# Scores of the last half block: two pairs to a bank, two teams in place of four

## The chip, the cores and the metric

The kernel runs on one core of one Trainium2 chip. The metric is the device time of one execution in microseconds (us). Engines are named as the profile names them: PE (TensorE matmul), PEld (its weight loads), DVE (VectorE), ACT (ScalarE), POOL (GpSimd), SP (SyncE, which issues most DMAs). Times written without a unit are microseconds from the start of the span.

## The reference

An attention without softmax feeds a mixture of experts whose router takes the best expert and keeps the first 768 tokens of each.

```python
scores = scale * np.matmul(z, z.transpose(0, 2, 1))        # 8 batches x 3072 x 3072, d_qk = 64, scale = 1 / 3072
attn = np.maximum(scores, 0.0) ** 2
x = u * np.matmul(attn, v)                                 # 24576 tokens x 256
...
logits = x @ w_gate                                        # 8 experts
expert_idx = np.argmax(logits, axis=1)
...
# the first capacity = 768 tokens of an expert, in order of the tokens, are kept; all others give rows of zeros
h = np.maximum(np.einsum('ecd,edf->ecf', disp, w1), 0.0)   # 256 -> 1024
y = np.einsum('ecf,efd->ecd', h, w2)                       # 1024 -> 256
out[i] = gate_w[i] * y[expert_idx[i], pos[i]]
```

## The kernel before

Numbers are carried as pairs of f16 (a high part and the rest), so that a product is three matmuls: high x high, high x rest, rest x high.

**Attention.** Only as many tokens are computed as fill the experts: 13 blocks of 512 queries and a last half block of 256, numbered 0 to 13. A block's keys come in 12 pairs of 128-key tiles. For a pair that isn't kept from an earlier block (scores are symmetric), `team` makes the scores with matmuls of 64 rows (`zz` by `zz` into the PSUM tiles `sc`, three for each tile, the two tiles of a pair on the two halves of the PE array), and `follow` lays out what happens to them: ACT takes the relu out of PSUM (`r`), ACT squares it (`a`), DVE casts the square to f16 and subtracts to get the rest (`hl`). The sums (`acc`) then take 12 matmuls of 256 columns for a pair of a half block. The tag `sc` has six banks of PSUM. Scores are made ahead of the sums for a team of pairs at a time, at most `TEAM = 3`, one bank for each tile; the list `teams` holds them in order, and `scores_to` starts a team when the sums come within two or three pairs of it. In block 13 pairs 0 and 1 are turned scores of block 12 (`nx`) and pairs 2 to 11 are computed: ten pairs.

**Routing.** When a block's sums are done, `drain` multiplies them by `u` (`x`), and `route` splits x into f16 parts (`rm`, `rse` ... for the scale, then `xr`), turns them with DMA transposes (`xt`), takes the logits on PE (`lg`, which takes one of the six banks too), counts slots (`cum`) and scatters the rows (`disp`) from POOL. Block 12 is routed while block 13 is computed, block 13 under the first expert's work.

**Experts.** A slab of an expert's rows is loaded (`fxt`, `meta`). For each of 8 groups of hidden columns PE makes `hps` in the banks of tag `sc`, and ACT and then DVE write its two f16 parts (`hh`). Then PE makes `yps`, which ACT and DVE scale (`ys`) and POOL scatters to `out`. The first slab has 640 rows in two halves of 384 and 256, so its hidden work is 16 groups of 6 matmuls; a bank comes free when DVE has written the group's `hh`. Weights are loaded (`wraw`), their largest value found (`wm`, an all-reduce on POOL, then `w1e` to `winv`) and split (`wt`). Expert 1's weights are prepared during block 13 and the first slab. Zero rows of the output are written between (`zero`).

**Order.** Nothing is scheduled on the chip: each engine runs its list in order. The list is made by the program itself: the PE work is written out in sequence, and `weave` puts in the steps of all waiting chains by an estimate of the engines' clocks (`clk`, with the costs written beside each step), the chain's rank, and conditions such as "six `hl` buffers". A change of one step's place or cost can therefore move steps of other chains on DVE, ACT and SP.

```python
blocks = [(bats[n // BPB], n % BPB, 0, CC if n < NB0 - 1 else CC // 2) for n in range(NB0)]
```

Of the kernel before, what the change touches and what calls it, by code (L numbers as in the profile page):

```python
# [9 lines left out]
F32 = mybir.dt.float32  # L10
# [8 lines left out]
P = 128  # L19
BLK = 512  # L20
MROW = 8
NHL = 6
TEAM = 3
# [5 lines left out]
def attention_moe_kernel(ctx: ExitStack, tc: tile.TileContext, u, v, z, w_gate, w1, w2, out, cap):  # L29
    nc = tc.nc  # L30
    B, S, D = u.shape
    DQ = z.shape[2]
# [4 lines left out]
    NPAIR = JT // 2  # L37
    BPB = S // BLK
    NBLK = B * BPB
    CC = BLK // P  # L40
# [11 lines left out]
    ps = ctx.enter_context(tc.tile_pool(name="ps", bufs=2, space=PSUM))  # L52
# [142 lines left out]
    def op(eng, cost, dep=0.0):  # L195
        start = max(clk[eng], dep + HOP)
        if eng in ("SP", "XB"):
            start = max(clk["SP"], dep + HOP)
            clk["SP"] = start + (0.5 if eng == "SP" else max(1.2, 0.3 + cost))
            clk["DMA"] = max(clk["DMA"], start + 1.4) + cost  # L200
            return clk["DMA"] + 1.0
        clk[eng] = start + cost
        return clk[eng]
# [64 lines left out]
    def weave():  # L268
        more_ = True
        while more_:  # L270
            more_ = watch()
            for c in list(chains):
                while c.fits():
                    c.emit()
                    more_ = True
                if c.item() is None:
                    chains.remove(c)

    def need(*keys):

        for k in keys:
            n = 0
            while k not in done:
                weave()
                if k not in done:
                    clk["PE"] += 0.1
                    n += 1
                    assert n < 100000, k
        return max((done[k] for k in keys), default=0.0)
# [573 lines left out]
    def attention(blocks, hook):  # L863
# [19 lines left out]
        def at(p):  # L883
            n, i = divmod(p, NPAIR)
            return n, 2 * order[n][i // 2] + i % 2

        def is_kept(p):
            n, g = at(p)
            bt, ib, _, _ = blocks[n]
            return (g // 2, ib) in bt.kept  # L890

        def is_next(p):


            n, g = at(p)
            bt, ib, _, _ = blocks[n]
            return (g // 2, ib) in bt.follows
# [8 lines left out]
        def cornered(p):  # L906


            n, g = at(p)
            _, ib, _, cc = blocks[n]  # L910
            return n > 0 and cc == CC and g == 2 * ib + 1


        computed = [p for p in range(NP) if not is_kept(p) and not is_next(p)]
        place = {p: i for i, p in enumerate(computed)}
        opening = hasattr(blocks[0][0], "to_scores")
        k = 6 if opening else 0
        teams = deque(tuple(computed[i:i + 2]) for i in range(0, k, 2))
        teams.extend(tuple(computed[i:i + TEAM]) for i in range(k, len(computed), TEAM))
        loads = deque(p for p in range(NP) if is_kept(p))  # L920

        def load(p):
# [12 lines left out]
        def team(ps_):  # L935

            made = []
            while small[0]:  # L940
                weave()
                clk["PE"] += 0.1 if small[0] else 0.0
            latest[:] = [0, *((aid, "r", place[p]) for p in ps_)]
            op("PE", 0.205)
            for p in ps_:
                n, g = at(p)
                bt, ib, c0, cc = blocks[n]
                t = need(bt.key("z", 2 * g // 4), bt.key("z", ib))
                if place[p] >= TEAM:
                    t = max(t, need((aid, "r", place[p] - TEAM)))  # L950
                w, q0 = cc * P, ib * BLK + c0 * P
                if cornered(p):
                    w, q0 = HB, q0 + HB
                s = [ps.tile([P, BLK], F32, tag="sc", name="sc", bufs=6) for _ in range(2)]
                for i, (kl, ql) in enumerate(((0, 0), (0, 1), (1, 0))):
                    for jj in (0, 1):
                        rows, j = slice(DQ * jj, DQ * (jj + 1)), 2 * at(p)[1] + jj
                        nc.tensor.matmul(s[jj][:, 0:w], lhsT=bt.zz[rows, (kl + jj) % 2, j * P:(j + 1) * P],  # L958
                                         rhs=bt.zz[rows, (ql + jj) % 2, q0:q0 + w], start=(i == 0), stop=(i == 2))
                t = op("PE", 3 * w / 2400, t)  # L960
                made.append(follow(p, s, w, t))
            return made

        def follow(p, s, w, t):
# [73 lines left out]
        def scores_to(p):  # L1038
            while teams and due() <= p:
                team(teams.popleft())  # L1040
# [52 lines left out]
        bt = blocks[0][0]  # L1093
        if hasattr(bt, "to_scores"):
            bt.to_scores()
            del bt.to_scores
            ahead = deque(teams[1])
            bt.to_sums(team(teams.popleft()), lambda: team((ahead.popleft(),)))
            teams.popleft()
        else:  # L1100
            scores_to(0)
        clear[0] = open_bank
        operand = {}
        for p, c in steps():
            where[:] = p, c
            n, g = at(p)
            bt, ib, c0, cc = blocks[n]
            i = p % NPAIR
# [18 lines left out]
            if i == 0 and c % 2 == 0:  # L1127

                k = bank[0] - 2
# [6 lines left out]
            for jj in (0, 1):  # L1136
                j = 2 * g + jj


                for h, l in ((0, 0), (0, 1), (1, 0)):  # L1140
                    nc.tensor.matmul(o, lhsT=a(h, jj, c), rhs=bt.v2[:, j, l], start=(i + jj + h + l + c % 2 == 0),  # L1141
                                     stop=(i == NPAIR - 1 and jj + h == 2), skip_group_check=True)
# [233 lines left out]
    with tc.manual_schedule():  # L1376
# [5 lines left out]
        for b, bt in bats.items():  # L1382
            n = min(BPB, NB0 - b * BPB)
# [55 lines left out]

        blocks = [(bats[n // BPB], n % BPB, 0, CC if n < NB0 - 1 else CC // 2) for n in range(NB0)]  # L1440
        attention(blocks, hook)
        done["attended"] = clk["PE"]
        cn = last_route[0][1]
# [16 lines left out]
        with tc.If(flag > 0):  # L1460
            nb, ib0 = divmod(NB0, BPB)

            def tail(b, ibs, half=()):
                go_on = nc.values_load(more, min_val=0, max_val=1)
                with tc.If(go_on > 0):
                    bt = batch(b)
                    prepare(bt)
                    attention([(bt, ib, CC // 2, CC // 2) for ib in half] + [(bt, ib, 0, CC) for ib in ibs],
                              lambda p: None)
                    finish()  # L1470
                    check_full()
                    finish()

            if ib0:
                tail(nb, range(ib0, BPB), [ib0 - 1])
                nb += 1
            else:
                tail(nb - 1, [], [BPB - 1])
            if nb < B:
                with tc.For_i(nb, B, 1) as b:  # L1480
                    tail(b, range(BPB))
            with tc.For_i(0, E, 1) as e:
                experts([e])
                finish()
# [25 lines left out]
```

## Time and profile before

| What | Value |
|---|---|
| Median of three runs | 777.61 us (776.28 to 780.22) |
| The profiled execution | 778.41 us, of which its span is 776.5 us |
| PE busy | 766.8 us, 99% of the span |
| DVE, ACT, POOL busy | 514.4, 401.1, 116.6 us |
| Block 13, from its first scores to the first `hps` | 494.54 to 519.49 |
| Hidden work of the first slab | 519.49 to 532.65 |

The span runs from the first to the last instruction of the profiled execution; its time is 1.9 us longer. In a row of the timeline the columns are the start, the time taken, the engine, the line, the operation, out<-in, the shapes and the count, and in brackets the idle time before it with what ended it. Ends of matmuls are modelled, so the time of PE's work is best read from one row's start to the next row's.

### The profile page before, as it was taken

How to read it: one execution, taken by the hardware profiler on the slowest of the kernel's cores; microseconds unless marked ns; L12 is line 12 of the kernel's file. 1: busy time of each engine (PE TensorE's matmuls, PEld its weight loads, DVE VectorE, ACT ScalarE, POOL GpSimd, SP SyncE). 2: the span in 40 equal slices, each digit the busy share in tenths (PEclk: the TensorE clock that was granted, in tenths of full speed). 3: DMA queues.
4: the chain of work that ended last, by engine and by line, in shares of the span. 5: the costliest groups of instructions: out<-in, count | busy, mean ns of one | idle time of the engine just before them, and what ended most of it. 6: DMA issues, size and time to landing. Idle time of an engine off the chain costs nothing.

```text
span 776.5 us, 16291 instructions
## 1 busy us (share of the span) xinstructions
PE 766.8 (99%) x6474; PEld 572.3 (74%) x6474; DVE 514.4 (66%) x1134; ACT 401.1 (52%) x690; POOL 116.6 (15%) x122
## 2 busy tenths in 40 slices
PE   9999999999999999999999999999999999999996
PEld 3777878888887787878888877876666656666664
DVE  7998789754308799875554268889576575575741
ACT  6985558433016667573530057675455464463541
POOL 0000020210202020202022020203320321313302
PEclk9999999999999999999999999999999999999999
DMA  7699949999978979698789949882898955944001
GB/s 224 124 351 137 288 104 241 178 220 195 189 149 166 326 177 228 164 235 190 166 153 197 201 134 214 305 233 58 236 264 286 319 147 215 296 120 185 28 15 45
DMA packets 283831, 149.49 MB, mean 193 GB/s; under 512 B 229742, under 2 KB 255675, under 8 KB 283745
## 3 DMA queue, kind: packets, MB, share of 16 engines
q1 hardware_dynamic: 278848, 135.57, 71.8%
q0 software_dynamic: 4896, 12.79, 5.3%
q8 instruction: 52, 0.85, 0.4%
q14 instruction: 35, 0.28, 0.1%
HBM read 36.25 MB, written 59.92 MB: 124 GB/s over the span
## 4 chain that ended last, share of the span: by engine, by line
PE 88%; issue 3%; DMA 3%; DVE 2%; POOL 1%; SPq 1%; ACT 0%; POOLq 0%; ACTq 0%; DVEq 0%
PE acc L1141 51%; PE hps L1287 14%; PE yps L1311 14%; PE sc L958 8%; DMA ld<-kept 2%; DMA vraw<-in_v 1%; POOL out L86 1%; PE lg L722 1%; DVE hl L993 1%; SPq L375 0%; DVE hl L984 0%; DVE wm L75 0%; DVE xr L707 0%; DVE v L527 0%; SPq L369 0%
## 5 line engine op out<-in xcount | busy, mean ns | idle before, releaser
L1141 PE MATMUL acc<-v,hl 128*128 128x256 f16 x2280 | 260.7, 273 | 1.0 <-DVE v L527 0.6
L1141 PEld LDWEIGHTS <-hl 128*128 128x128 f16 x2280 | 219.5, 98 | 36.4 <-issue 9.2
L975 ACT ACTIVATE r<-sc 128x512 f32<-128x512 f32 (+1 forms) x212 | 105.5, 550 | 142.2 <-PE sc L958 140.0
L1311 PE MATMUL yps<-wt,hh 128*128 128x256 f16 (+1 forms) x776 | 126.8, 324 | 0.0
L1287 PE MATMUL hps<-fxt,wt 128*128 128x384 f16 (+2 forms) x816 | 126.7, 317 | 0.0
L993 DVE TENSOR_TENSOR hl<-a,hl 128x1024 f16<-128x1024 f32 (+1 forms) x106 | 118.1, 1114 | 3.5
L1287 PEld LDWEIGHTS <-wt 128*128 128x128 f16 x816 | 77.8, 98 | 47.1
L1311 PEld LDWEIGHTS <-hh 128*128 128x128 f16 x776 | 75.7, 98 | 48.4
L86 POOL DMA_INDIRECT disp<-xr,slot x54 | 56.8, 1051 | 359.7 <-issue 215.5
L1141 PE MATMUL acc<-v,ld 128*128 128x256 f16 x960 | 109.0, 273 | 0.6 <-DMA ld<-kept 0.6
L980 ACT ACTIVATE a<-r 128x1024 f32<-128x1024 f32 (+1 forms) x106 | 102.6, 968 | 5.0 <-DVE hl L993 2.6
L1141 PEld LDWEIGHTS <-ld 128*128 128x128 f16 x960 | 92.7, 98 | 13.9 <-issue 2.1
L984 DVE CAST hl<-a 128x1024 f16<-128x1024 f32 (+1 forms) x106 | 67.5, 637 | 45.8 <-ACT a L980 45.0
L1273 DVE SCALAR_TENSOR_TENSOR hh<-hps,hh 128x384 f16<-128x384 f32 (+2 forms) x136 | 70.6, 530 | 34.6 <-ACT hh L1272 33.1
L1272 ACT ACTIVATE hh<-hps 128x384 f16<-128x384 f32 (+2 forms) x136 | 63.4, 470 | 48.9 <-PE hps L1287 47.3
L86 POOL DMA_INDIRECT out<-ys,sid x48 | 53.3, 1111 | 129.9 <-DVE ys L1320 77.1
L958 PE MATMUL sc<-zz 64*128 64x512 f16 (+1 forms) x636 | 68.5, 355 | 0.0
L704 ACT ACTIVATE xr<-x,rsr 128x256 f16<-128x256 f32 x54 | 24.4, 500 | 82.9 <-DVE rsr L62 66.7
L1317 ACT ACTIVATE ys<-yps,sg 128x256 f32<-128x256 f32 x48 | 22.7, 474 | 76.9 <-PE yps L1311 70.4
L1320 DVE SCALAR_TENSOR_TENSOR ys<-yps,sg,ys 128x256 f32<-128x256 f32 x47 | 22.7, 483 | 53.0 <-ACT ys L1317 50.6
L1141 PE MATMUL acc<-v,nx 128*128 128x256 f16 x504 | 57.4, 273 | 0.0
L1141 PEld LDWEIGHTS <-nx 128*128 128x128 f16 x504 | 49.0, 98 | 6.5 <-issue 0.8
(135 smaller groups left out, 485.7 us busy)
## 6 DMA issues: line engine op xcount, KB each, us to landing
out<-zero SPq DMA_DIRECT2D x48, 512.0 KB
kept<-hl SPq DMA_DIRECT2D x40, 512.0 KB
wraw<-in_moe_w SPq DMA_DIRECT2D x32, 512.0 KB
vraw<-in_v SPq DMA_DIRECT2D x18, 512.0 KB
u<-in_u SPq DMA_DIRECT2D x13, 512.0 KB
zraw<-in_z SPq DMA_DIRECT2D x2, 768.0 KB
zz<-zz SPq DMA_DIRECT2D x4, 384.0 KB
xt<-xr SPq DMA_TRANSPOSE x54
```

Of the source, the lines that this page charges most:

```text
L86: r = nc.gpsimd.indirect_dma_start(out=dst, out_offset=bass.IndirectOffsetOnAxis(ap=idx, axis=0), in_=src, in_offset=None, bounds_check=bo ...
L704: return lambda: nc.scalar.activation(st.x16[:, c, 0:D], st.x[:, c, :], AF.Copy, scale=st.rs[:, c:c + 1])
L958: nc.tensor.matmul(s[jj][:, 0:w], lhsT=bt.zz[rows, (kl + jj) % 2, j * P:(j + 1) * P], rhs=bt.zz[rows, (ql + jj) % 2, q0:q0 + w], start=(i ...
L975: nc.scalar.activation(sct[p][:, jj, :], s[jj][:, 0:w], AF.Relu)
L980: nc.scalar.activation(sq[p], sct.pop(p), AF.Square)
L984: nc.vector.tensor_copy(hl[:, :, :, 0, :], sq[p].rearrange("p j (t k) -> p j t k", k=HB))
L993: nc.vector.tensor_sub(hl[:, :, :, 1, :], a.rearrange("p j (t k) -> p j t k", k=HB), hl[:, :, :, 0, :])
L1141: nc.tensor.matmul(o, lhsT=a(h, jj, c), rhs=bt.v2[:, j, l], start=(i + jj + h + l + c % 2 == 0), stop=(i == NPAIR - 1 and jj + h == 2), sk ...
L1272: Chain([[("ACT", 0.05 + w * 0.00083, lambda: nc.scalar.activation(th, src, AF.Relu), None)], [("DVE", 0.07 + w * 0.00104, lambda: nc.vect ...
L1273: [("DVE", 0.07 + w * 0.00104, lambda: nc.vector.scalar_tensor_tensor(out=tl, in0=src, scalar=0.0, in1=th, op0=ALU.max, op1=ALU.subtract), ...
L1287: nc.tensor.matmul(o, lhsT=wx.w1[:, d, wp, f * P:(f + 1) * P], rhs=sx.xt[:, xp * DC + d, a:a + w], start=(q == 0), stop=(q == len(seq) - 1))
L1311: nc.tensor.matmul(y[:, 0 if end else l], lhsT=hid(i, f)[:, sl], rhs=w[:, l], start=(f + i == 0 and l != 1), stop=(f == FC - 1 and i == 1) ...
```

## The change

In the half block two pairs share two banks: the first tiles of both lie side by side in one bank of 2 x 256 columns, the second tiles in another. The matmuls of the two pairs are interleaved (all three products of both), the first of a bank clears it. A team may then hold twice as many pairs as six banks allowed before, and the ten pairs are made in two teams of five. Full blocks keep their teams; their tiles are given the width that they use.

```diff
-        teams.extend(tuple(computed[i:i + TEAM]) for i in range(k, len(computed), TEAM))
+        full = sum(blocks[p // NPAIR][3] == CC for p in computed)
+        if full > k:
+            teams.extend(tuple(computed[i:min(i + TEAM, full)]) for i in range(k, full, TEAM))
+        k = -(-(len(computed) - full) // (2 * TEAM))
+        n = -(-(len(computed) - full) // max(k, 1))
+        teams.extend(tuple(computed[i:i + n]) for i in range(full, len(computed), max(n, 1)))
...
-                s = [ps.tile([P, BLK], F32, tag="sc", name="sc", bufs=6) for _ in range(2)]
+                if cc == CC:
+                    s = [ps.tile([P, 1, w], F32, tag="sc", name="sc", bufs=6) for _ in range(2)]
+                    two = [(p, 0)]
+                elif ps_.index(p) % 2 == 0:
+                    s = [ps.tile([P, 2, w], F32, tag="sc", name="sc", bufs=6) for _ in range(2)]
+                    two = [(x, y) for y, x in enumerate(ps_[ps_.index(p):ps_.index(p) + 2])]
+                else:
+                    two = []
                 for i, (kl, ql) in enumerate(((0, 0), (0, 1), (1, 0))):
-                    for jj in (0, 1):
-                        rows, j = slice(DQ * jj, DQ * (jj + 1)), 2 * at(p)[1] + jj
-                        nc.tensor.matmul(s[jj][:, 0:w], lhsT=bt.zz[rows, (kl + jj) % 2, j * P:(j + 1) * P],
-                                         rhs=bt.zz[rows, (ql + jj) % 2, q0:q0 + w], start=(i == 0), stop=(i == 2))
-                t = op("PE", 3 * w / 2400, t)
-                made.append(follow(p, s, w, t))
+                    for x, y in two:
+                        for jj in (0, 1):
+                            rows, j = slice(DQ * jj, DQ * (jj + 1)), 2 * at(x)[1] + jj
+                            nc.tensor.matmul(s[jj][:, y], lhsT=bt.zz[rows, (kl + jj) % 2, j * P:(j + 1) * P],
+                                             rhs=bt.zz[rows, (ql + jj) % 2, q0:q0 + w], start=i + y == 0, stop=i == 2,
+                                             skip_group_check=True)
+                for x, y in two:
+                    made.append(follow(x, [z[:, y] for z in s], w, op("PE", 3 * w / 2400, t)))
```

Up to the half block every engine's list is as it was. From there the planner places other chains differently. Two places matter for what follows.

On SP, while block 13 is computed, the list before has expert 1's weights (`wraw`) ahead of the first slab (`fxt`), and then the turning of block 12's rows (`xt`):

```order
L1071 DMA u<-in_u 128x4x256
L1399 DMA out<-zero 256x1x512 x3
L1172 DMA wraw<-in_moe_w 128x1024 x2
L1174 DMA wraw<-in_moe_w 128x4x256 x2
L1399 DMA out<-zero 256x1x512
L1241 DMA_TRANSPOSE fxt<-disp 128x4x640
L1242 DMA meta<-disp 128x5x8
L1399 DMA out<-zero 256x1x512 x3
L715 DMA_TRANSPOSE xt<-xr 128x4x128 x4
```

The same place of the list after the change:

```order
L1085 DMA u<-in_u 128x4x256
L1413 DMA out<-zero 256x1x512 x3
L1255 DMA_TRANSPOSE fxt<-disp 128x4x640
L1256 DMA meta<-disp 128x5x8
L1186 DMA wraw<-in_moe_w 128x1024 x2
L1188 DMA wraw<-in_moe_w 128x4x256 x2
L1413 DMA out<-zero 256x1x512 x2
L715 DMA_TRANSPOSE xt<-xr 128x4x128 x2
```

The slab, which waits for the scatters of block 11, now stands ahead of the four weight loads, and the loads stand ahead of the turning of block 12's rows.

On DVE, around the first hidden groups of the first slab, the list before goes from the end of block 13 (`x<-acc`) over the seven small steps for expert 1's scale to the first `hh`, and has the routing of block 13 between the groups:

```order
L1080 TENSOR_TENSOR x<-acc,u 128x512
L60 TENSOR_SCALAR w1e<-wma 128x1
L62 TENSOR_SCALAR w1i<-w1e 128x1
L62 TENSOR_SCALAR w1r<-w1i 128x1
L60 TENSOR_SCALAR w2e<-wma 128x1
L62 TENSOR_SCALAR w2i<-w2e 128x1
L62 TENSOR_SCALAR w2r<-w2i 128x1
L1198 TENSOR_TENSOR winv<-w1i,w2i 128x1
L1273 SCALAR_TENSOR_TENSOR hh<-hps,hh 128x384
L1273 SCALAR_TENSOR_TENSOR hh<-hps,hh 128x256
L692 TENSOR_REDUCE rm<-x 128x2
```

After the change the seven steps come first, then `x<-acc`, and then these rows; the first `hh` stands behind the routing steps of block 13 up to `xr` and two splits of expert 1's weights:

```order
L692 TENSOR_REDUCE rm<-x 128x2
L60 TENSOR_SCALAR rse<-rm 128x2
L62 TENSOR_SCALAR rsi<-rse 128x2
L62 TENSOR_SCALAR rsr<-rsi 128x2
L60 TENSOR_SCALAR rf<-rsi,cb 128x2
L60 TENSOR_SCALAR rfg<-rsi,cbg 128x2
L1228 SCALAR_TENSOR_TENSOR wt<-wraw,w1r,wt 128x512
L770 COPY xr<-tokid 128x2x4
L60 TENSOR_SCALAR tokid<-tokid 128x4
L1228 SCALAR_TENSOR_TENSOR wt<-wraw,w1r,wt 128x512
L707 SCALAR_TENSOR_TENSOR xr<-x,rsr,xr 128x256 x2
L1287 SCALAR_TENSOR_TENSOR hh<-hps,hh 128x384
```

Behind the first `hh` now come the six steps on block 12's logits (`lgs` to `oh`), which before stood ahead of `x<-acc`. On PE the logits of block 12 (`lg`, 16 matmuls) moved from the last sums of block 13 to behind the second hidden group, and those of block 13 (8 matmuls) from the `yps` work into the ninth group.

## Rows read from the trace of the kernel before

**Rows 1.** The page, parts 1 and 2: PE's busy time, granted clock.

```profile
PE 766.8 (99%) x6474; PEld 572.3 (74%) x6474; DVE 514.4 (66%) x1134; ACT 401.1 (52%) x690; POOL 116.6 (15%) x122
PEclk9999999999999999999999999999999999999999
```

**Rows 2.** The timeline of PE in block 13 and the first slab.

```profile
494.54 1.16 PE L958 MATMUL sc<-zz 64*128 64x256 f16 x18
495.63 4.10 PE L1141 MATMUL acc<-v,hl 128*128 128x256 f16 x36
499.57 2.78 PE L1141 MATMUL acc<-v,nx 128*128 128x256 f16 x24
...
512.69 0.50 PE L958 MATMUL sc<-zz 64*128 64x256 f16 x6
513.12 4.53 PE L1141 MATMUL acc<-v,hl 128*128 128x256 f16 x38
...
518.76 0.55 PE L722 MATMUL lg<-wg,xt 128*128 128x16 f16 x16
519.16 0.49 PE L1141 MATMUL acc<-v,hl 128*128 128x256 f16 x3
519.49 6.03 PE L1287 MATMUL hps<-fxt,wt 128*128 128x384 f16 x42
...
532.65 0.81 PE L1311 MATMUL yps<-wt,hh 128*128 128x512 f16 x4
```

**Rows 3.** The timeline of ACT behind block 13's first scores.

```profile
495.14 0.66 ACT L975 ACTIVATE r<-sc 128x256 f32<-128x256 f32 x2 [3.15 <-PE sc L958]
...
496.49 0.66 ACT L975 ACTIVATE r<-sc 128x256 f32<-128x256 f32 x2
```

**Rows 4.** The timeline of DVE at the end of block 13 and after.

```profile
514.52 2.34 DVE L75 TENSOR_REDUCE wm<-wraw 128x1 f32<-128x1024 f32 x2
516.78 0.42 DVE L984 CAST hl<-a 128x512 f16<-128x512 f32 x1
...
517.84 0.15 DVE L1188 TENSOR_REDUCE wm<-wm 128x2 f32<-128x4 f32 x1
519.34 0.22 DVE L733 TENSOR_REDUCE lgs<-lg 128x32 f32<-128x64 f32 x1 [1.35 <-PE lg L722]
...
520.60 0.68 DVE L1080 TENSOR_TENSOR x<-acc,u 128x512 f32<-128x512 f32 x1
521.21 0.14 DVE L60 TENSOR_SCALAR w1e<-wma 128x1 int32<-128x1 int32 x1
...
522.15 0.88 DVE L1273 SCALAR_TENSOR_TENSOR hh<-hps,hh 128x384 f16<-128x384 f32 x2
522.94 0.68 DVE L692 TENSOR_REDUCE rm<-x 128x2 f32<-128x512 f32 x1
...
524.33 0.16 DVE L60 TENSOR_SCALAR rse<-rm 128x2 int32<-128x2 int32 x1
...
525.07 0.88 DVE L1273 SCALAR_TENSOR_TENSOR hh<-hps,hh 128x384 f16<-128x384 f32 x2
...
525.96 0.16 DVE L770 COPY xr<-tokid 128x8 f32<-128x8 f32 x1
...
526.24 0.75 DVE L1214 SCALAR_TENSOR_TENSOR wt<-wraw,w1r,wt 128x512 f16<-128x512 f32 x1
526.90 0.48 DVE L707 SCALAR_TENSOR_TENSOR xr<-x,rsr,xr 128x256 f16<-128x256 f32 x1
```

**Rows 5.** The timeline of DVE where it waits for an all-reduce of POOL.

```profile
481.92 0.15 DVE L60 TENSOR_SCALAR w1e<-wma 128x1 int32<-128x1 int32 x1 [0.50 <-POOL wma L79]
```

**Rows 6.** The timeline of SP's queue (SPq) in block 13.

```profile
489.41 2.52 SPq L1172 DMA_DIRECT2D wraw<-in_moe_w  x2
...
503.83 2.44 SPq L1241 DMA_TRANSPOSE fxt<-disp  x1
...
509.25 7.44 SPq L715 DMA_TRANSPOSE xt<-xr  x4
```

## The prediction

> **What bounds the kernel now.** The page comes first: PE is busy for 766.8 of a span of 776.5 us and its granted clock is full in all forty slices [rows 1]. Work that PE doesn't do costs nothing unless it makes PE wait, so the change is worth what it takes off PE's list, plus the waits it ends, less the waits it makes. Before the half block the lists are the same. So I lay the timeline of PE from the first scores of block 13 to the end of the first slab's hidden work [rows 2] beside the new lists, and take the other engines' timelines for how long their steps hold them.
>
> Start to start, one sum takes (499.57 - 495.63) / 36 = 0.1094 us. A team of 18 score matmuls takes 495.63 - 494.54 = 1.09, one of 6 takes 513.12 - 512.69 = 0.43; so 12 more cost 0.66, and a team costs 0.10 by itself. Block 13 and the last sums of block 12, from 494.54 to 519.49, are 24.95 us [rows 2]. Work in it by these prices: 180 sums 19.69, three teams of 18 and one of 6 3.70, the logits 519.16 - 518.76 = 0.40; together 23.79. The other 1.16 us is PE waiting for scores to become sums' operands: between 513.12 and 518.76 there are 45 sums (38 in that row, 7 in one not shown), 4.92 us of work in 5.64.
>
> **The change part by part.**
>
> *Fewer teams.* A team of 30 takes 1.09 + 0.66 = 1.75; two take 3.50 in place of 3.70. Gain 0.20 us.
>
> *The waits in block 13.* With teams of five, scores start earlier relative to their use. The first relu began 0.60 after its team (495.14), with 5 of 6 matmuls done [rows 2, 3]; now the two pairs' matmuls are interleaved and it can begin after 11 of 12, 0.33 later by 0.66 for 12. From pair to pair ACT took 496.49 - 495.14 = 1.35 [rows 3]. PE by the new list: team 494.54 to 496.29, 36 sums to 500.23, 24 on the turned scores to 502.86, 24 to 505.49, second team to 507.24, 96 sums to 517.74. The second team's relus begin at 505.49 + 0.60 + 0.33 = 506.42, its five squares end every 1.35, later by about 0.45 each for the two splits of block 12 that stand between them on ACT: 507.8, 509.1, 510.9, 512.6, 513.9. DVE needs 517.84 - 516.78 = 1.06 for a pair [rows 4], so the last is ready at 515.0. PE wants these five from 511.18 on in steps of 1.31, the last at 516.4; 1.4 us of room. I take the waits as gone. Block 13's sums end at 517.74; with the logits, which now follow among the hidden groups, that is 518.14 against 519.49. **Gain 1.35 us** (0.20 of it is the teams). Bounds: all of it, or 0.2 if all waits stay.
>
> *The first slab's hidden groups.* PE has six banks. Groups 1 to 5 and block 12's logits take them; group 6 needs the bank of group 1 back, thus the first `hh` of DVE. Before, that came at 522.15, in time. Now DVE does more ahead of it, from the last pair at 515.0 [rows 4, 5]: two `wm` 516.78 - 514.52 = 2.26; small `wm` 0.15; the all-reduce, 0.50 of waiting; seven small steps 522.15 - 521.21 = 0.94; `x` 0.61; `rm` 0.68; scale 525.07 - 524.33 = 0.74; two splits of weights, 526.90 - 526.24 = 0.66 each; token numbers 0.28; two `xr` 0.96. Sum 8.44, so the first `hh` starts at 523.4. It takes 0.44 and its narrower neighbour 0.36 (two of them 522.94 - 522.15 = 0.79), and the bank is back at 524.0.
>
> PE meanwhile: 96 hidden matmuls took 532.65 - 519.49 = 13.16, which is 0.99 for a group of 384 columns and 0.66 for one of 256. From 517.74 the five groups and the logits take 3 x 0.99 + 2 x 0.66 + 0.40 = 4.69, to 522.4. Group 6 waits 1.6. Group 7 needs the second `hh`, which stands behind the six steps on the logits (520.60 - 519.34 = 1.26): 523.4 + 0.44 + 1.26 + 0.36 = 525.5, so it starts at 525.6, another 0.9 late. From there to group 13 PE has 4.93 of groups 7 to 12 and about 0.35 of small matmuls, to 530.9; group 13 needs the ninth `hh`, and DVE has in front of its end nine `hh` 3.6, two sets of logit steps 2.52, three splits 1.98: 8.1, so 531.5, and the group starts 0.7 late. Four groups, 3.3, end at about 534.9. Before, the same point with block 13's logits was 532.65 + 0.20 = 532.85. **Net loss 2.1 us**, in which the gain of 1.35 is already spent: the waits in the slab are some 3.4 us.
>
> *The SP queue.* Four weight loads go behind the slab, which was issued at 503.83 because of its scatters [rows 6]. With a full queue a load takes 2.52 / 2 = 1.26. If the slab is issued no earlier, block 12's turning starts at 509.25 + 4 x 1.26 less one zero fill (about 1.2), 513.1, and if its four DMAs again take 7.44, they are out at 520.5 and landed by 522.6 (before, 516.69 out, and PE took the logits at 518.76 without a wait of its own). PE comes to the logits at 517.74 + 1.65 = 519.4. So from nothing to 3.2 us of waiting; but PE would wait 1.6 and 0.9 behind it anyway, so up to about 2 hides there. The lower end, nothing: without the loads ahead of them the scatters should land sooner and the slab be issued sooner, and a queue that isn't full takes a load faster. I take nothing for it.
>
> *Costs of nothing.* Block 13's logits come earlier than before; block 12's rows are scattered a few us later, but block 13's scatters stand behind them either way and are no later, and the next slab to need them is two slabs on. Behind the first slab the PE list is the same to within a few places.
>
> The sum against its own time: the profiled execution took 778.41, its span and 1.9 around it, so 780.5. It lies 0.8 above the median of 777.61; on the median the forecast is **779.7 us**.
>
> **Rivals.**
>
> *DVE is in time (faster).* All of the loss hangs on when DVE reaches the first `hh`. Group 13's wait vanishes if that is 3.2 earlier, and the net is zero where it starts at 521.5, two us before my time; with no wait left the result is 1.35 us of gain, 776.3. For it: my chain adds up steps each behind the other, and the reduces could start as soon as DVE idles between pairs. Against: a list is done in order, and squares come every 1.35 to 1.8 us.
>
> *SP is late.* The weights and turned rows come at the end of their range and their scatter of DMAs fills the queue: `wm` waits, then `lg`, then block 13's own turning behind four zero fills and the next slab. About 1.5 to 4 us on top: 781 to 784.
>
> *The clock falls.* PE would stand three times within 10 us at the start of the slab. If that took the clock from 2.4 to 1.2 GHz, the work between, groups 6 to 16, some 8.5 us, could take as much again: up to 788. No slice of the profile shows a lower clock [rows 1], though this stretch had no such waits. The Trainium skill ("TensorE: Matmul & The Clock Gate", "HAM oscillation — how this bites in real kernels") describes kernels whose PE falls back to the lower clock in each wait for data. By that rule the result would lie at the upper end of this rival; the trace neither bears it out nor excludes it.
>
> That the change doesn't do what it says is excluded by the new list, which has two teams.
>
> **How the numbers follow.** My forecast, 778.2 to 781.5: 0.58. DVE in time, 776 to 778.2: 0.23. SP late, 781 to 784: 0.14. Clock: 0.03. Something else: 0.02. A measurement of this kernel tells about 0.5%, 3.9 us, from no change. Slower than 781.5 are most of the SP case and the clock case, 0.14; faster than 773.7 nothing here reaches, 0.02; the rest is 0.84. The range leaves out the lower edge of the fast case and the upper of the slow ones: 776.6 to 782.6.
>
> **What would show it.** Right: two teams of 30 matmuls, PE without waits from 494.54 until about 517.7, then `hps` with waits that end with `hh` of DVE at the sixth, seventh and thirteenth group, `yps` starting near 535; behind it every stretch as before, moved by about 2 us. Wrong: waits of PE on operands `hl` between 507 and 517 (the gain isn't there), a wait at `lg` that ends with a DMA (the SP case), a slice with a lower granted clock, or a first `hh` before 522. What I may have overlooked is a wait further on, at the slabs whose rows are scattered later.

## The result, and the profile after

The change takes 781.93 us (median of 7 runs, 780.89 to 783.0), the kernel before, run beside it, 777.87 (7 runs, 776.28 to 780.22). The ratio is 1.0053, 95% interval 1.0037 to 1.0069: slower by 2.9 to 5.4 us. The profiled execution took 781.04, its span is 779.2.

The page of the changed kernel, parts 1 and 2, answers to [rows 1]:

```profile
PE 766.2 (98%) x6474; PEld 573.1 (74%) x6474; DVE 514.5 (66%) x1134; ACT 400.9 (51%) x690; POOL 116.2 (15%) x122
...
PEclk9999999999999999999999999999999999999999
```

PE does the same work in a longer span, at the full clock. Its timeline from block 13 to the second slab answers to [rows 2] (columns as there; in brackets the wait and what ended it):

```profile
493.30 1.81 PE L971 MATMUL sc<-zz 64*128 64x256 f16 x30
495.04 4.10 PE L1155 MATMUL acc<-v,hl 128*128 128x256 f16 x36
...
504.31 1.81 PE L971 MATMUL sc<-zz 64*128 64x256 f16 x30
506.06 10.65 PE L1155 MATMUL acc<-v,hl 128*128 128x256 f16 x96
516.55 1.79 PE L1301 MATMUL hps<-fxt,wt 128*128 128x384 f16 x12
518.18 0.35 PE L722 MATMUL lg<-wg,xt 128*128 128x16 f16 x8
518.96 0.26 PE L722 MATMUL lg<-wg,xt 128*128 128x16 f16 x4 [0.44 <-DMA xt<-xr]
519.38 0.26 PE L722 MATMUL lg<-wg,xt 128*128 128x16 f16 x4 [0.16 <-DMA xt<-xr]
519.49 2.77 PE L1301 MATMUL hps<-fxt,wt 128*128 128x384 f16 x18
523.70 2.93 PE L1301 MATMUL hps<-fxt,wt 128*128 128x256 f16 x21 [1.44 <-DVE hh L1287]
527.37 0.26 PE L722 MATMUL lg<-wg,xt 128*128 128x16 f16 x4 [0.74 <-DMA xt<-xr]
528.04 0.26 PE L722 MATMUL lg<-wg,xt 128*128 128x16 f16 x4 [0.41 <-DMA xt<-xr]
...
534.31 2.76 PE L1325 MATMUL yps<-wt,hh 128*128 128x512 f16 x16
...
547.38 2.11 PE L1301 MATMUL hps<-fxt,wt 128*128 128x384 f16 x12
549.76 6.01 PE L1301 MATMUL hps<-fxt,wt 128*128 128x384 f16 x36 [0.26 <-issue]
555.60 7.96 PE L1325 MATMUL yps<-wt,hh 128*128 128x512 f16 x48
```

The second slab of the kernel before, to compare with the last three rows:

```profile
546.04 7.96 PE L1287 MATMUL hps<-fxt,wt 128*128 128x384 f16 x48
553.84 7.96 PE L1311 MATMUL yps<-wt,hh 128*128 128x512 f16 x48
```

Start to start, a team of 30 takes 1.74 and 1.75, and block 13 has no wait: 516.55 - 493.30 = 23.25 us. All that is lost stands behind it. DVE in the same stretch, for [rows 4]:

```profile
518.36 0.69 DVE L1094 TENSOR_TENSOR x<-acc,u 128x512 f32<-128x512 f32 x1 [0.64 <-PE hps L1301]
...
523.09 0.55 DVE L1287 SCALAR_TENSOR_TENSOR hh<-hps,hh 128x384 f16<-128x384 f32 x1
523.56 0.21 DVE L733 TENSOR_REDUCE lgs<-lg 128x32 f32<-128x64 f32 x1
```

And SP's queue, for [rows 6]:

```profile
504.51 0.93 SPq L1188 DMA_DIRECT2D wraw<-in_moe_w  x2
505.49 1.25 SPq L1413 DMA_DIRECT2D out<-zero  x2
506.91 4.31 SPq L715 DMA_TRANSPOSE xt<-xr  x2
...
512.36 3.63 SPq L715 DMA_TRANSPOSE xt<-xr  x2
516.04 4.06 SPq L1413 DMA_DIRECT2D out<-zero  x4
520.20 3.16 SPq L1255 DMA_TRANSPOSE fxt<-disp  x1
...
524.17 2.52 SPq L715 DMA_TRANSPOSE xt<-xr  x2
```

Block 13's rows were split by 523.2 (two `xr` from 522.30, 0.88 us), but their turning was issued at 524.17, behind four zero fills and the next slab.

The books, from block 13's first scores to the end of the span: before 776.5 - 494.54 = 281.96, after 779.2 - 493.30 = 285.90, so +3.94 us, close to what the medians say (+4.06). They are opened at these scores because the time ahead of them differs between executions: in the traces of the runs below the scores begin between 493.57 and 499.00, in e5 at 494.82 and in e7 at 499.00 with the same lists ahead of them. The logits (0.40 and 0.20) are taken out where they stand:

| Stretch | Before | After | Difference |
|---|---|---|---|
| Block 13, without logits | 24.55 | 23.25 | -1.30 |
| First slab, hidden work, without logits | 13.16 | 17.16 | +4.00 |
| First slab, `yps`, without logits | 13.19 | 13.07 | -0.12 |
| Second slab, hidden work | 7.80 | 8.22 | +0.42 |
| Third slab, hidden work | 2.71 | 3.07 | +0.36 |
| From the start of the last scatter to the end | 5.76 | 6.34 | +0.58 |

The stretches between are the same to 0.02. All of these are readings of one trace of each kernel.

### The profile page after: what moved, and what is told of

It is laid out like the page before. It is cut to its first block, busy times and chain, and to the rows that moved or that the text cites. A ratio compares the mean times of both kernels' runs of the same rounds, so it can differ in the third digit from the quotient of the medians.

```text
span 779.2 us, 16287 instructions
## 1 busy us (share of the span) xinstructions
PE 766.2 (98%) x6474; PEld 573.1 (74%) x6474; DVE 514.5 (66%) x1134; ACT 400.9 (51%) x690; POOL 116.2 (15%) x122
## 4 chain that ended last, share of the span: by engine, by line
PE 91%; issue 3%; DMA 2%; DVE 1%; POOL 1%; SPq 1%; ACT 0%; POOLq 0%; DVEq 0%; ACTq 0%
PE acc L1155 55%; PE yps L1325 14%; PE hps L1301 14%; PE sc L971 8%; DMA vraw<-in_v 1%; POOL out L86 1%; PE lg L722 1%; SPq L375 0%; DMA xt<-xr 0%; DVE hl L1007 0%; DVE v L527 0%; SPq L369 0%; DVE hh L1287 0%; ACT junk L1197 0%; ACT xr L704 0%
```

## The experiments

Theory A, mine: the gain in block 13 is real, and the loss is made by two lists that the planner wrote anew around it. DVE comes late to the first `hh` (group 6 waits), and SP comes late to the turned rows (both `lg` wait). Rival B: two pairs in a bank, or five pairs of scores at once, cost by themselves. Rival C: SP and the DMA alone; DVE only waits beside it. Each run was timed in turn with the kernel before on the same chip, so what counts is the ratio to before (the change: 1.0053).

**e1: shared banks, but four teams.**

```diff
-        k = -(-(len(computed) - full) // (2 * TEAM))
-        n = -(-(len(computed) - full) // max(k, 1))
+        k = -(-(len(computed) - full) // TEAM)
+        n = TEAM
```

> Two pairs still share banks in the half block, but its ten pairs are made in four teams (3, 3, 3, 1) again; the planner then gives DVE, ACT and SP the lists of before, so this isolates the sharing of banks from the moved lists. If the lists are the cause of the loss (the wait for the first hh and the turned rows), the time is that of before, 777.9 within 1, block 13 takes 24.6 to 25.2 from first scores to first hps, and group 6 and both lg wait for nothing. If sharing a bank itself costs (later relus, or matmuls that are slower on a bank that is read), block 13 is longer than 25.5 and the time is 779 or more.

Measured: 778.91 against 778.57, ratio 1.0002 (0.9982 to 1.0022). PE's timeline:

```profile
493.57 1.16 PE L971 MATMUL sc<-zz 64*128 64x256 f16 x18
...
516.68 0.94 PE L1155 MATMUL acc<-v,hl 128*128 128x256 f16 x7 [0.34 <-DVE wm L1202]
...
518.19 6.03 PE L1301 MATMUL hps<-fxt,wt 128*128 128x384 f16 x42
...
531.35 0.81 PE L1325 MATMUL yps<-wt,hh 128*128 128x512 f16 x4
```

Block 13 takes 24.62 with its logits (before 24.95), the slab's hidden work 13.16 as before. Sharing a bank costs nothing that can be measured; the first half of B falls. That 24.62 is 0.33 less than before shows no gain of the shared banks by itself, since block 13 of the kernel before differs as much between traces: with the same lists of PE, ACT and DVE up to there it took 24.95 in the trace above, 24.84 in e6 and 24.30 in e3, by the waits in it. With two teams it took 23.25 or 23.26 in every run that has them. So the gain of 1.30 is that against one trace; against that of e3 it is 0.65.

**e2 and e3: block 13's routing held back by 8 us**, in the change (e2) and in the kernel before (e3).

```diff
-                xs.pop(n), bt, max(done[k] for k in keys), LAG if n < len(blocks) - 1 else 0.5, cc, rid, follows,
+                xs.pop(n), bt, max(done[k] for k in keys) + (8.0 if n == len(blocks) - 1 and straight[0] else 0.0), LAG if n < len(blocks) - 1 else 0.5, cc, rid, follows,
```

> The change, with the routing of block 13 (rm to xr) held back by 8 us in the planner, so that DVE comes to the first hh right behind x and one or two splits of weights; PE's list is the same through block 13 and the SP list is the same up to block 13's turning. If DVE's list is the cause: the first hh starts near 3 us earlier after the first scores, group 6 doesn't wait for hh (1.6 us less), block 13's lg, which now comes in the yps work or later, doesn't wait (1.45 less), block 12's lg still waits 0.9 for its turned rows; the time is 778.9, and 1 us above before is what later slabs and that wait leave. If the SP queue is the cause and DVE only waits beside it: PE waits as long for xt as it did for hh, and the time stays within 1 of 781.9.

> The same edit to the kernel before (four teams, routing of block 13 held back by 8 us). It tells whether holding the routing back is worth something by itself. In the kernel before the first hh was in time and no bank was waited for, so both theories expect 777.9 within 1, with hidden work of the first slab again near 13.2. If it comes out 2 us faster, a gain of the run before this one is not the repair of the change but of something the kernel before has too.

e2: 780.56 against 778.57, ratio 1.0018 (1.0002 to 1.0035). Group 6 and block 13's `lg` no longer wait; block 12's `lg` still does, by 0.9, as expected. But four splits of weights moved up in front of the first `hh` (525.09, 5.09 behind the last sum; in the change 6.54), and two later groups wait for `hh`, 1.1 together from start to start. The first slab has 2.0 of waits in place of 4.0. Most of what went is the 1.45 of block 13's `lg`, which now stands in the `yps` work; of the 1.6 for `hh` only 0.5 went. C falls for group 6, which no longer waits though SP's list up to there is the same; how much of the loss is DVE's, this run doesn't tell.

e3 did not stay put: 781.95 against 778.57, ratio 1.0032 (1.0017 to 1.0047). Its first slab is that of before (13.17), but PE stands 3.73 us at the fourth slab, for `fxt`, whose rows of block 13 were turned and scattered later:

```profile
570.71 2.77 PE L1287 MATMUL hps<-fxt,wt 128*128 128x384 f16 x9 [3.73 <-DMA fxt<-disp]
```

So holding the routing back by 8 us is no free repair, and e2 is no clean measure of DVE's share.

**e4: expert 1's scale and splits held back** to the third group of columns.

```diff
                 act(o, hid(0, f)[:, a:a + w], hid(1, f)[:, a:a + w], w, (fid, "h", f, i))
+                if f == 2 and straight[0]:
+                    done.setdefault("attended", clk["PE"])
...
         attention(blocks, hook)
-        done["attended"] = clk["PE"]
```

> The change, with expert 1's scale and splits held back until the third group of columns of the first slab; block 13's routing stays ahead of the first hh. This takes the all-reduce's wait, seven small steps and two splits, 0.5 + 0.94 + 1.3 us, out of DVE's way to the first hh, though part of it lay under the wait for the end of block 13's sums (x waits for PE either way). If the place of DVE in its list is the cause, the first hh starts 1.3 to 1.5 us earlier and the wait of group 6 falls from 1.6 to at most 0.3; the wait of block 13's lg for turned rows falls by as much only if it hangs on xr and not on the queue; time 780.0 to 780.6. If the SP queue is the cause, no change: 781.9, with lg13 waiting 1.4 as before.

Measured: 783.82 against 778.57, ratio 1.0061 (1.0039 to 1.0083): no faster than the change (1.0053) and not to be told apart from it, where A had 780.0 to 780.6. PE:

```profile
523.54 2.45 PE L1301 MATMUL hps<-fxt,wt 128*128 128x256 f16 x18 [0.79 <-DVE hh L1287]
528.07 0.28 PE L722 MATMUL lg<-wg,xt 128*128 128x16 f16 x4 [2.08 <-DMA xt<-xr]
528.62 0.27 PE L722 MATMUL lg<-wg,xt 128*128 128x16 f16 x4 [0.27 <-DMA xt<-xr]
```

and its windows (the window and its length, then the busy time of PE, PEld, DVE, ACT and POOL, the granted clock, the DMA share, GB/s):

```profile
527.00:528.00 1.00, 0.00 (x0) 0.00 (x0) 1.00 (x3) 1.00 (x4) 0.00 (x0) 1.00 0.97 198
528.00:529.00 1.00, 0.66 (x9) 0.42 (x10) 0.80 (x3) 0.32 (x2) 0.00 (x0) 0.52 0.41 148
529.00:530.00 1.00, 1.00 (x5) 0.47 (x4) 0.83 (x6) 0.00 (x0) 0.00 (x0) 0.50 1.00 377
530.00:531.00 1.00, 1.00 (x5) 0.58 (x4) 0.49 (x2) 0.14 (x1) 0.00 (x0) 0.50 0.02 4
```

The first `hh` comes 29.11 behind the first scores, 0.7 earlier than in the change and not the 1.3 to 1.5 expected, since `x` waits for PE as long as there. The wait for `hh` falls to 0.9 from start to start (in the change 1.6), DVE's part as A has it, in half of the size expected. But block 13's logits go on 528.07 - 493.83 = 34.24 us behind the first scores, in the change 527.37 - 493.30 = 34.07: that moment is SP's, which issued the turning 30.89 behind the first scores (in the change 30.87), though `xr` was 0.7 earlier. What group 6 gave back, `lg` took (2.4 in place of 1.2 by the brackets, with three matmuls fewer ahead of it). And after a wait of 2.08 the granted clock was 0.50 (1.2 GHz) for some three microseconds; the nine hidden matmuls behind took 2.7 in place of 1.3. So both queues bind, one behind the other, and relieving DVE's alone gains nothing here.

**e5 and e6: the zero fills begun one block earlier**, in the change and in the kernel before (where the lists of PE, DVE and ACT stay the same).

```diff
-            if n >= (NB0 - 1) // BPB * BPB and g < NPAIR - 4 and zq:
+            if n >= NB0 - 3 and g < NPAIR - 4 and zq:
```

> The change, with the zero fills of the output begun one block earlier, so that none is left on SP at the end of block 13: block 12's turning follows the weight loads at once, the next slab follows block 13's u and the turning, and block 13's turning has no zero fills ahead of it. The planner then also puts block 12's lg into the fifth hidden group and the first two hh of DVE behind only x, rm and five scale steps. Two causes are held (DVE's list before the first hh, and SP's list before the turned rows): then both lg wait for nothing, and the first hh, at 1.8 + 0.7 + 0.7 + 0.8 = 4.0 us behind the last sum, gives group 6, due at 4.7, a wait of at most 0.2; the first slab's hidden work falls from 17.8 to 13.7 to 14.2 and the time is that of before or up to 1.3 below it (777.3 to 778.6 where before is 778.6). If the loss lies in what five pairs' scores at once do to ACT and DVE, no order gives it back: still 3 us or more above before.

> The same edit to the kernel before, as a control: the lists of PE, DVE and ACT stay word for word, only SP's zero fills come a block earlier. No wait of the kernel before hangs on them, so both theories expect the time of before within 1. If it is faster by more than 1, the zero fills cost the kernel before something too and the gain of the run above isn't the repair of the change; if slower, the earlier fills collide with the rows that block 12's sums load.

e6: 779.46 against 779.04, ratio 1.0003 (0.9989 to 1.0018), as expected. e5 repairs the first slab altogether: hidden work 13.77 with both logits, where 13.76 is without a wait. It moves DVE's steps as well, as expected above, so it doesn't relieve SP alone. Yet the time is 782.35 against 779.04, ratio 1.0048 (1.0031 to 1.0065). The loss had moved: the second slab's hidden work takes 11.40 in place of 7.80, from the first to the second of these rows of PE:

```profile
544.91 5.69 PE L1301 MATMUL hps<-fxt,wt 128*128 128x384 f16 x34
...
556.31 8.18 PE L1325 MATMUL yps<-wt,hh 128*128 128x512 f16 x48
```

All engines of e5 there:

```profile
545.02 0.97 POOL L86 DMA_INDIRECT disp<-xr,slot  x1 [0.30 <-issue]
546.30 0.97 POOL L86 DMA_INDIRECT disp<-xr,slot  x1 [0.31 <-issue]
547.58 0.99 POOL L86 DMA_INDIRECT out<-ys,sid  x1 [0.30 <-issue]
548.67 0.48 ACT L1331 ACTIVATE ys<-yps,sg 128x256 f32<-128x256 f32 x1 [5.29 <-PE hps L1301]
548.87 0.97 POOL L86 DMA_INDIRECT out<-ys,sid  x1 [0.30 <-issue]
...
551.72 0.48 PE L1301 MATMUL hps<-fxt,wt 128*128 128x384 f16 x2 [1.12 <-issue]
...
551.77 1.64 ACT L1286 ACTIVATE hh<-hps 128x384 f16<-128x384 f32 x4 [2.62 <-remote]
```

ACT's `hh` had its data since 546, and PE stands within a group; both go on within 0.05 us, released by nothing of the program that the profile names, during and behind a row of ten scatters that POOL issues one behind the other (537.08 to 549.84). The clock was at 0.50 from 554 to 556 as well, behind that stand. The change has a trace of this itself: its ACT, idle for 6.89, goes on at 549.82, PE at 549.76 (its line stands above). The profile puts ACT's wait down to PE there, but PE stood for only 0.26.

```profile
549.82 0.84 ACT L1331 ACTIVATE ys<-yps,sg 128x256 f32<-128x256 f32 x2 [6.89 <-PE hps L1301]
```

**e7 and e8: both repairs**, zero fills earlier and the routing held back by 2 us (e7) or 3 us (e8): the diffs of e5 and of e2 with 2.0 and 3.0.

> Both repairs: zero fills a block earlier, and block 13's routing held back by 2 us in the planner, so that the first two hh stand right behind x and the seven small steps, ahead of rm. First hh at 1.8 + 0.7 + 0.9 = 3.4 us behind the last sum; no hidden group and no lg waits; hidden work of the first slab 13.56 to 13.8; the gain of block 13, 1.3, is left over, less up to 0.8 in the later slabs: 0.5 to 1.3 below before. The rival (the loss is the change's own) expects 3 us or more above before.

> As the run above with the routing held back by 3 us: block 13's rm stands behind the third hh, its lg in the yps work, where the kernel before has it. No wait in the first slab; the scatters of block 13 come up to 1 us later than in the run above. If 8 us of delay cost the fourth slab a late load (a wait of 3.7 in the run that held the routing back in the kernel before), 3 us should still be free: 0.5 to 1.3 below before.

e7: 779.23 against 779.04, ratio 1.0006 (0.9993 to 1.0018); e8: 780.31, ratio 1.0022 (1.0007 to 1.0037). In both the first slab is free of waits (13.77, and 13.57 with one `lg` in it) and block 13 takes 23.25. The second slab takes 8.51 and 9.70, with ACT and PE going on 0.06 us apart again. Rival B is done with: with five pairs at once as before, other orders give 2.4 to 3.7 us back (the ratios against the change's). Both runs had been expected 0.5 to 1.3 below the kernel before and missed that: the second slab takes back 0.7 (e7) and 1.9 (e8).

**e9 to e12: what makes the second slab stand.** e9 (on e5) and e12 (on the change) leave out the five scatters of the first slab's output; e10 (on e5) and e11 (on e7) issue them behind block 13's scatters. In each only POOL's list differs from its base.

```diff
-                   [("POOL", 1.04, lambda t=t: scatter("out", out, tid[:, t:t + 1], ys[t], NTOK - 1), None)]],
+                   [("POOL", 1.04, (lambda: None) if n == 640 and straight[0] else lambda t=t: scatter("out", out, tid[:, t:t + 1], ys[t], NTOK - 1), None)]],
```

```diff
-                   [] if end else [("DVE", 0.4, add, (fid, "y", t))],
-                   [("POOL", 1.04, lambda t=t: scatter("out", out, tid[:, t:t + 1], ys[t], NTOK - 1), None)]],
+                   [] if end else [("DVE", 0.4, add, (fid, "y", t))]] + ([] if n == 640 and straight[0] else [[("POOL", 1.04, lambda t=t: scatter("out", out, tid[:, t:t + 1], ys[t], NTOK - 1), None)]]),
                   -1, clk["PE"])
+            if n == 640 and straight[0]:
+                watchers.append((lambda k=(fid, "y", t): k in done, lambda t=t, k=(fid, "y", t): Chain(
+                    [[("POOL", 1.04, lambda: scatter("out", out, tid[:, t:t + 1], ys[t], NTOK - 1), None)]], 4, done[k] + 10.0)))
```

> The kernel with zero fills a block earlier, now without the five scatters of the first slab's 640 output rows (those rows of the output stay zero); the lists of PE, DVE, ACT and SP are word for word the same. With the scatters, the first slab was repaired (13.8) but the second slab's hidden work took 11.4 in place of 7.8: ACT and PE went on at the same moment with nothing named that they waited for, while POOL issued ten scatters one behind the other. If that unbroken row of scatters, or the buffers ys that they give back, holds ACT up: the second slab takes 7.8 to 8.0 and the time falls by 3.4, to between 1.3 below before and 1 above it. If the stall comes from anything else (the loading of instructions, the banks, the place of ACT's steps): 11 again, and 3.3 above before.

> The same kernel with all its scatters, the five of the first slab held behind block 13's two on POOL; only POOL's list differs (six scatters of turned rows, then all of the output, in place of 4, 2, 2 and 3). If ACT waits for buffers ys that a scatter gives back, they come back later: the stall grows past 3.6 or starts earlier. If it is the unbroken row of scatters as such, it stays at 3 to 4 and the time 3 above before. If it is the order (output rows between the rows of blocks 12 and 13), it goes: within 1 of before.

> The kernel with zero fills a block earlier and the routing 2 us later, which lost 0.7 in its second slab, with the scatters of the first slab held behind block 13's. If the order of the scatters makes the stall, the second slab takes 7.8 and the whole 0.7 to 1.3 less than before. If ACT waits for buffers that scatters give back, the second slab is longer than 8.5 and the time 1 or more above before. If neither, 8.5 again and the time of before within 0.7.

> The change itself, without the five scatters of the first slab's 640 output rows (those rows stay zero); no other list differs. It prices the part of the change's loss that sits behind the first slab: 0.4 in the second and 0.4 in the third. If POOL's scatters, which the change moved 4 us later and together, make these, both go and the time is 0.8 below that of the change, 3.2 above before; the waits of the first slab (4.0: group 6 for hh, both lg for turned rows) stay. If they come from elsewhere: 4 above before, with second and third slab at 8.2 and 3.1 again.

| Run | Time, before beside it | Ratio (interval) | Second slab |
|---|---|---|---|
| e9 | 777.88, 778.19 | 0.9994 (0.9978 to 1.0011) | 7.80 |
| e10 | 778.99, 778.19 | 1.0008 (0.9992 to 1.0024) | 7.80 |
| e11 | 778.20, 778.19 | 0.9994 (0.9977 to 1.0011) | 7.80 |
| e12 | 782.60, 778.19 | 1.0054 (1.0037 to 1.0071) | 7.80 |

The scatters make the stand (e9, where no other list differs from e5's), and it is enough to issue the first slab's output behind block 13's rows (e10, e11): held, they were issued from 550.3 on in e11, behind a gap of 5.5 us in POOL's row. That ACT waits for buffers that they give back is excluded: held longer, the wait goes, and the first slab's five `ys` take five of the six buffers of their tag. e10 lost 1.7 elsewhere, in the fourth slab (8.27 and 9.04 in place of 7.80 twice, a wait for `hh`); that stands at the same place in e2 and, with the lists of before, in e6 and (0.6) in e1, so it isn't the change's alone. e12 puts the scatters' part of the change's own loss at the 0.42 of its second slab; the 0.36 of the third stays (3.06), the first slab has its waits (17.95 with the logits), and the time doesn't move. The 0.8 expected was twice too much.

PE in e11, which has no wait left:

```profile
495.69 1.81 PE L971 MATMUL sc<-zz 64*128 64x256 f16 x30
...
518.94 3.91 PE L1301 MATMUL hps<-fxt,wt 128*128 128x384 f16 x27
...
532.71 3.74 PE L1325 MATMUL yps<-wt,hh 128*128 128x512 f16 x22
...
546.05 7.96 PE L1301 MATMUL hps<-fxt,wt 128*128 128x384 f16 x48
553.85 7.96 PE L1325 MATMUL yps<-wt,hh 128*128 128x512 f16 x48
```

From the first scores to the end of its span it takes 776.4 - 495.69 = 280.71, before 281.96: 1.25 less by these two traces, nearly all of the gain of block 13. That is 0.16% and lies within the interval of the timed runs; e11 beats the change by some 4.6 us, the kernel before by nothing that can be told.

## Why the prediction was right, and where not

The forecast was 779.7; 781.93 lies in its range, above the band of its own case (778.2 to 781.5) and in that of the rival "SP is late" (781 to 784).

- **Fewer teams, 0.20:** right (1.74 and 1.75 for a team, predicted 1.75).
- **The waits in block 13:** right. Block 13 took 23.25, predicted 517.74 - 494.54 = 23.20; the gain was 1.30, predicted 1.35. The waits that it ends are 1.16 in the one trace that the sum was made from, but only 0.5 in that of e3.
- **First `hh` of DVE:** the mechanism was right, its time 0.9 late: 29.8 behind the first scores, predicted 28.9. 0.64 of it is `x`, which by the profile waited for PE until twelve hidden matmuls were through, a wait that the sum did not have. It begins 1.81 behind the start of these matmuls, in e4 1.79, but in e5, where `lg` stands further back in PE's list, 0.20; why it waits for them stays open.
- **Group 6 waits 1.6:** measured 1.6, but by two misses that cancel: `hh` came 0.9 later, and PE came to the group 0.9 later, since block 12's `lg` had waited that long. e5 and e7 confirm the cause: with `hh` in time the wait is gone.
- **Groups 7 and 13 wait 0.9 and 0.7:** wrong, neither waited. Group 7 began while the second `hh` was still to come (524.82), after `lgs` (523.56) had read block 12's logits; so by these times it had their bank, not that of group 2. The sum also counts some 0.13 of `cum` matmuls twice on the way to group 13, which are in the 13.16 already.
- **"The SP queue", "I take nothing for it":** the step that failed. Block 12's `lg` waited 0.9, within the span of 0 to 3.2 and hidden in group 6's wait as said. Block 13's `lg` waited 1.45, hidden behind nothing: its turning stood behind four zero fills and the next slab, which I had put into the rival alone. e4 pins it to SP, and with e5's lists it is gone. A wait at `lg` that ends with a DMA was among the prediction's own signs of being wrong.
- **"Costs of nothing" in the later slabs:** wrong by 0.8 (second 0.42, third 0.36), and 0.58 lie behind the last scatter. e12 gives the second slab to POOL's scatters. In the third, 0.20 is a wait for `hh` of DVE. The third slab's loss and the 0.58 are there in e4 (3.09; 6.29) and e12 (3.06; 6.45) as well and not in e2, e5, e7 and e8 (2.75 or 2.76; 5.56 to 5.72), so they go with the change's order; why, stays open.
- **The clock:** it did not fall in the change. The windows around its longest stands:

```profile
521.00:524.00 3.00, 1.56 (x12) 0.96 (x11) 2.86 (x9) 3.00 (x8) 0.00 (x0) 1.00 1.05 391
...
527.00:528.00 1.00, 0.26 (x4) 0.17 (x4) 1.00 (x3) 0.17 (x1) 0.00 (x0) 1.00 0.44 90
```

The rival was nearer than its 0.03 says: in e4 the clock fell behind a wait of 2.08. The Trainium skill ("TensorE: Matmul & The Clock Gate", "HAM oscillation — how this bites in real kernels") describes a kernel whose PE falls back to the lower clock in each wait for data. The traces agree with it for the waits of 2.08 and 3.73 and not for those of up to 1.45. That kernel's waits are longer than those in the prediction's sum, so the page was no reason to put this result at the rival's upper end.

So the sum was short by 0.6 in the first slab (waits of 4.0 for 3.4), by 0.8 behind it and by 0.6 at the end of the span. That the first slab came out so near is partly luck: 1.6 of the waits forecast for `hh` did not come, and 2.35 at `lg`, which the sum had at nothing, stood in their place. Of the mechanism, the two teams, the end of the waits in block 13 and DVE's late first `hh` were right; SP and the later slabs were not.

## What to carry to other kernels

Where a planner writes the lists, price an edit by what it does to every list: here 1.3 us were gained where the edit stands (against one trace of before) and 5.2 lost behind it, at least 4.4 of them in lists of DVE, SP and POOL that it never named. A wait that goes gives its time to the next late thing (DVE, then SP's turning, then POOL's scatters), so repairs have to be tried together and followed to the end of the span. An edit that is worth 0.16% at best needs its neighbours' order pinned before it can pay.

## What the runs showed of the hardware that was not expected

- POOL's scatters of output rows, issued between those of turned rows, held ACT and PE up in the change, e5, e7 and e8 (second slab 8.22 to 11.40 in place of 7.80), though the profile names no wait of either engine for them. PE goes on first and ACT 0.05 to 0.06 us behind it, 2.3 to 2.9 us after the start of the last scatter issued. Without these scatters, or with them held back, the stand is gone. e2 and e4 had ten scatters in a row too, e2 in the very order of e5, and their second slab took 7.80, so neither a long row nor the order suffices alone. By which way the scatters reach ACT and PE stays open.
- PE's granted clock fell to 0.50 behind stands of 3.73 us (e3), 2.08 (e4) and, in pieces, about 2 (e5), and cost 1.4 to 1.7 us on top in e3 and e4. Behind waits of up to 1.45 in the change it stayed at 1.00.
- DMA transposes of turned rows took longer to issue with zero fills just ahead of them in SP's queue: four took 7.44 us in the kernel before, with three zero fills ahead, and 5.34 in e6 without; two and two took 4.31 and 3.63 in the change, with two zero fills ahead, and 3.54 and 2.50 in e5, 4.01 and 2.66 in e7, without.
